# The third group of the second layer joins the seven products in blocks 2 to 5, and exp and relu work in G

## The chip, the cores and the metric

The kernel runs on one core of one Trainium2 chip. The metric is the device time of one execution in microseconds; the runs shown have a median of 294.54 us (294.45 to 295.62, three runs). Engines are named as in the profile: PE is TensorE (PEld its weight loads), DVE is VectorE, ACT is ScalarE, POOL is GpSimd, and SP is the engine whose queue issues most DMAs.

## The reference

The inputs are q, k and v of 8 batches, 8 heads, 576 positions and 64 columns, and two weight matrices. A linear attention feeds a two-layer network:

```
q_s = softmax of q over the columns          k_s = softmax of k over the positions
kv  = k_s^T v  (per head)                    x   = q_s kv, heads side by side: 4608 x 512
h   = x @ w_in            (512 x 2048)
g   = h where h > 0, else exp(h) - 1
out = g @ w_out           (2048 x 512)       4608 x 512, float32
```

## The kernel before

**Blocks.** The 4608 rows of x are cut into nine blocks (j = 0 to 8) of 512 rows. The attention of a batch is worked off in 16 half batches (n = 0 to 15): load q, k and v, exp on ACT, sums and normalisation (`stage1`), turning q by a DMA transpose (`turn`), widening (`widen`), the small matmuls (`side`, `kv_mm`, `ao_mm`), and a copy to XT (`xt`), where x lies transposed.

**First layer.** For each block, eight groups g = 0 to 7 of 256 hidden columns each. A group (`hg`, `hg_mm`) is eight matmuls of 512 columns into one half of PSUM's first four banks (`PS[g % 2]`), then exp on ACT from PSUM into a buffer ESB (two of them, in turn), relu(1 - exp) on ACT in ESB, and two DVE instructions that make max(h, 0) - relu(1 - exp) from PSUM and ESB and write it into two units of GR (here called G). So a PSUM half is free for the group after next when the second of these two is done. G has 24 units; a block takes 16 of them, 8 that the pair ts = 1 of the block before last has left and 8 that the pair ts = 0 of the last block has left (`units`).

**Second layer.** Blocks 0 and 1 do it with plain matmuls (`out_mm`). From block 2 on, a block has two pairs (ts = 0, 1) of 256 rows, and `pair` multiplies each by w_out in the manner of Winograd: 2 x 2 quarters, seven products in place of eight. The contraction of 2048 is cut into three groups, `GROUPS = ((0, 4), (4, 6), (6, 8))` in units z of 256. A product of a group is one 256-column matmul per z. The sums that the products need are made beforehand: differences of weights once (`combos`: T1 to T4, of which T2 to T4 in TB and T1 in place in W2), and four sums of G's quarters per pair and group (`sums`: S1 and A11 - A21; `late`: A11 - S1 and A12 less that), on POOL, each of (z1 - z0) x 128 columns.

In blocks 2 to 5 only groups 0 and 1 take part in the seven products (`groups(j)`); the third group (z = 6, 7) is done by `std`: four 512-column matmuls for each of the two 128-row tiles of a pair. From block 6 (`WHOLE`) on, the third group takes part too, with its weight differences in TB2 and its sum in SB2, two buffers that lie over RAW, free by then.

DVE adds the products up from PSUM (`dve` in `pair`, L871), ACT copies two quarters from PSUM (`copy`, L876), and SP stores the rows (`store`).

**Order.** Each engine's order is written out by hand as lists of operation numbers (`ORDER`, found by a planner beforehand). `Sched.add` notes what each operation reads and writes, and `emit` issues each engine's list in order with a semaphore wait where an operation depends on another engine's. So an engine works strictly in the order of its list: an operation that waits holds everything behind it. The planner's own times are used only to place a few warming matmuls at the start (`fill`).

Of the kernel before, what the change touches and what calls it, by code (L numbers as in the profile page):

```python
# [21 lines left out]
NSP = 6  # L22
# [78 lines left out]
class Op:  # L101
    __slots__ = ("eng", "dur", "emit", "deps", "key", "idx", "start", "end",
                 "dma", "sem", "val", "clock", "nbytes", "follow", "side", "late", "packet", "margin",
                 "gate", "span", "behind", "early")

    def __init__(self, eng, dur, emit, key, dma=None, nbytes=0):
        self.eng, self.dur, self.emit, self.key = eng, dur, emit, key
        self.deps = {}
        self.dma, self.nbytes = dma, nbytes
        self.start = self.end = None  # L110
        self.behind, self.early = None, 0
        self.follow, self.side, self.packet, self.margin = None, 0, 4608, 0


class Sched:
# [4 lines left out]
    LAND = 350  # L120
    SPIN_FROM, WARM = 5500.0, 11300.0
    FIRST = {"sp": 2050, "act": 2050, "gp": 2700}
    DMA_RATE = 385.0

    def __init__(self, nc):
        self.nc = nc
        self.E = {"sp": nc.sync, "act": nc.scalar, "dve": nc.vector,
                  "pe": nc.tensor, "gp": nc.gpsimd}
        self.ops = []
        self.w = {}  # L130
        self.r = {}
        self.gate = None

    def add(self, eng, dur, emit, key, R=(), W=(), X=(), dma=None, nbytes=0, after=(),
            follow=None, side=0):
        op = Op(eng, dur, emit, key, dma, nbytes)
        op.idx = len(self.ops)
        op.follow, op.side, op.late, op.gate = follow, side, False, self.gate
# [22 lines left out]
    def order(self):  # L161
        line = {e: [self.ops[int(i)] for i in ORDER[e].split()] for e in self.ENG}
        free = {e: 740.0 for e in self.ENG}
        queue = {e: 0.0 for e in self.ENG}
        seq = []
        while any(line.values()):
            before = len(seq)
            for e in self.ENG:
# [104 lines left out]
def t_f32r(n):  # L273
    return (n + 32) / 2.4
# [881 lines left out]
```

## Time and profile before

| | |
|---|---|
| median of three runs | 294.54 us |
| profiled execution, first to last instruction | 292.2 us, 5351 instructions |
| 8 matmuls of a first-layer group, L637 | 576 in all, 142.7 us busy |
| plain second layer, L698 (blocks 0 and 1) | 128, 32.4 us |
| seven products, L850 | 672 of 256 columns |
| third group, L863 (std) | 64 of 512 columns, 17.3 us |
| GR written on DVE, L676 | 120 of 512 columns, 689 ns each |
| adding products on DVE, L871 | 84, 417 ns each |
| exp and relu on ACT, L653 and L673 | 72 and 64, 1025 and 1060 ns each |
| sums on POOL, L798 | 256 columns some 745 ns, 512 columns some 1300 ns |
| longest waits | DVE for relu 55.7 us (46 times), ACT for the first layer's matmuls 36.9 us (43 times), DVE's adds for products 25.7 us (27 times) |
| loads of k, q, v on SP's queue, from issue to landing | 6.1, 5.0, 5.4 us in the median |

The page gives no time of the profiled execution beside its span; the median of the runs is 2.3 us above it. Waits of DVE, ACT and POOL cost nothing as long as PE does not wait for them in turn. Matmuls overlap, so a group's mean duration (393 ns for L637) is more than its share of time: 142.7 us for 576 is 248 ns each, and the distance between pieces of the chain is nearer still.

### The profile page before, as it was taken

Reading aid. Unit: us, or ns where it says so; the run is one execution under the profiler, and the core shown is the slowest. Engines: PE = TensorE matmul, PEld = TensorE weight load, DVE = VectorE, ACT = ScalarE, POOL = GpSimd, SP = SyncE. Lnnn points to the kernel's source line nnn. Section 1 sums busy time; section 2 is a strip of 40 time slices with the busy share of each in tenths; the row PEclk is TensorE's granted clock in tenths of the full one; section 3 lists DMA queues with packets and bytes.
Section 4 is the critical chain, followed back from the end, with each engine's and each line's share of the span. In section 5 each row is a group of like instructions: output and inputs, shape, how many; then the busy total and the mean of one; then the engine's idle time right before and its main releaser. Section 6 shows DMA issues by size and latency. Waiting matters only on the chain.

```text
span 292.2 us, 5351 instructions
## 1 busy us (share of the span) xinstructions
PE 282.1 (97%) x2128; PEld 242.1 (83%) x2128; DVE 177.4 (61%) x326; ACT 211.3 (72%) x249; POOL 220.6 (76%) x216
## 2 busy tenths in 40 slices
PE   2899999999999999999999999999999999999994
PEld 0478887778888888888988888988989889988994
DVE  3748834787464686575656675756542667356753
ACT  4858849988998989786976779856883667665610
POOL 1992435617788999899786979799678968899880
PEclk9999999999999999999999999999999999999999
DMA  7999999799995679577919476403111010400235
GB/s 254 397 367 388 389 389 335 169 281 332 274 316 125 101 232 159 168 182 254 234 45 207 150 157 202 98 16 77 38 36 36 2 31 5 110 0 2 55 90 144
DMA packets 36472, 50.01 MB, mean 171 GB/s; under 512 B 16352, under 2 KB 18144, under 8 KB 36448
## 3 DMA queue, kind: packets, MB, share of 16 engines
q1 hardware_dynamic: 29680, 33.96, 43.5%
q0 software_dynamic: 6528, 15.47, 17.6%
q10 hardware_dynamic: 240, 0.26, 0.4%
q8 instruction: 16, 0.26, 0.4%
q14 instruction: 8, 0.07, 0.1%
HBM read 36.70 MB, written 9.44 MB: 158 GB/s over the span
## 4 chain that ended last, share of the span: by engine, by line
PE 94%; DMA 2%; POOL 2%; SPq 0%; issue 0%; DVE 0%
PE PS L637 46%; PE PS L850 28%; PE PS L698 10%; PE PS L863 5%; PE PS L552 3%; DMA KR<-in_k_dram 2%; PE PS L521 2%; POOL W L379 1%; POOL VB L418 0%; PE PS L465 0%; POOL QS L441 0%; SPq L359 0%; PE PS L564 0%; DVE OSB L871 0%
## 5 line engine op out<-in xcount | busy, mean ns | idle before, releaser
L637 PE MATMUL PS<-XT,W 128*128 128x512 f32 x576 | 142.7, 393 | 0.1
L676 DVE SCALAR_TENSOR_TENSOR GR<-PS,ESB 128x512 fp32r<-128x512 f32 (+1 forms) x124 | 87.5, 705 | 59.6 <-ACT ESB L673 55.7
L637 PEld LDWEIGHTS PS<-XT,W 128*128 128x128 f32 x576 | 105.0, 188 | 21.5 <-DMA W<-in_moe_w_in_dram 0.5
L653 ACT ACTIVATE ESB<-PS 128x1024 f32<-128x1024 f32 x72 | 73.5, 1025 | 38.4 <-PE PS L637 36.9
L673 ACT ACTIVATE ESB<-ESB 128x1024 f32<-128x1024 f32 x64 | 67.8, 1060 | 1.5
L798 POOL TENSOR_TENSOR GR<-GR 128x512 fp32r<-128x512 f32 (+1 forms) x65 | 62.7, 982 | 5.5 <-PE PS L850 4.9
L871 DVE TENSOR_TENSOR OSB<-OSB,PS 128x256 f32<-128x256 f32 x84 | 34.6, 417 | 26.9 <-PE PS L850 25.7
L850 PE MATMUL PS<-W,GR 128*128 128x256 f32 x288 | 45.5, 284 | 0.0
L850 PE MATMUL PS<-TB,GR 128*128 128x256 f32 x288 | 43.8, 283 | 0.0
L441 POOL TENSOR_TENSOR QS<-QR,RZQ 128x1152 f16<-128x1152 f32 (+1 forms) x16 | 30.2, 1886 | 17.2 <-DVE RZQ L433 16.5
L850 PEld LDWEIGHTS PS<-W,GR 128*128 128x128 f32 x288 | 40.8, 190 | 2.0
L850 PEld LDWEIGHTS PS<-TB,GR 128*128 128x128 f32 x288 | 39.9, 191 | 1.7
L798 POOL TENSOR_TENSOR SB<-GR 128x256 fp32r<-128x256 f32 (+1 forms) x31 | 30.0, 973 | 11.4 <-DVE GR L676 10.4
L698 PE MATMUL PS<-W,GR 128*128 128x512 f32 x128 | 32.4, 395 | 0.0
L798 POOL TENSOR_TENSOR GR<-SB,GR 128x256 fp32r<-128x256 f32 (+1 forms) x31 | 29.9, 978 | 2.4 <-PE PS L850 1.9
L418 POOL CAST VB<-VR 128x1152 bf16<-128x1152 f32 (+1 forms) x16 | 17.7, 1106 | 16.1 <-DMA VR<-in_v_dram 16.1
L698 PEld LDWEIGHTS PS<-W,GR 128*128 128x128 f32 x128 | 23.4, 188 | 4.7 <-DVE GR L683 0.2
L430 DVE TENSOR_REDUCE ZQ<-QR 128x18 f32<-128x1152 f32 (+2 forms) x18 | 21.8, 1209 | 6.5 <-ACT QR L428 4.9
L586 ACT ACTIVATE XT<-PS 128x512 fp32r<-128x512 f32 (+6 forms) x32 | 19.2, 603 | 6.8 <-PE PS L552 3.0
L876 ACT ACTIVATE OSB<-PS 128x256 f32<-128x256 f32 x28 | 10.4, 377 | 18.3 <-PE PS L850 9.3
L402 ACT ACTIVATE KR<-KR 128x1152 bf16<-128x1152 f32 x16 | 18.4, 1157 | 0.8 <-DMA KR<-in_k_dram 0.8
L398 ACT ACTIVATE QR<-QR 128x1152 f32<-128x1152 f32 x14 | 16.3, 1161 | 1.5 <-DMA QR<-in_q_dram 1.5
(57 smaller groups left out, 220.4 us busy)
## 6 DMA issues: line engine op xcount, KB each, us to landing
out_dram<-OSB SPq DMA_DIRECT2D x61, 128.0 KB, 2.4
QR<-in_q_dram SPq DMA_DIRECT2D x12, 576.0 KB, 5.0
KR<-in_k_dram SPq DMA_DIRECT2D x12, 576.0 KB, 6.1
VR<-in_v_dram SPq DMA_DIRECT2D x12, 576.0 KB, 5.4
W<-in_moe_w_out_dram POOLq DMA_DIRECT2D x4, 1024.0 KB, 16.6
QR<-in_q_dram POOLq DMA_DIRECT2D x4, 576.0 KB, 12.1
VR<-in_v_dram POOLq DMA_DIRECT2D x4, 576.0 KB, 13.0
KR<-in_k_dram POOLq DMA_DIRECT2D x4, 576.0 KB, 11.1
```

The source lines that it names most:

```text
L402: S.add("act", t_act(1152, False), lambda e: e.activation(ek[:, :, :, :].rearrange("p h c d -> p (h c d)"), flat(k), AF.Exp), key - 2, X=[ ...
L430: S.add("dve", t_dve(m), lambda e, qp=qp, zp=zp: e.tensor_reduce(zp, qp, AX.X, ALU.add), key - 3, R=[f"qR{i}{x}" for x in xs], W=[f"ZQ{i}{ ...
L441: lambda e, qp=q[:, :, a:b, :], rz=rz, dst=qs[:, :, a:b, :]: e.tensor_tensor(dst, qp, rz, ALU.mult),
L586: S.add("act", t_act((h1 - h0) * n_, True), lambda e, dst=dst, src=src: e.activation(dst, src, AF.Copy), key, W=W, X=X)
L637: last = e.matmul(P[:, t * 512:(t + 1) * 512], self.W1[:, kc, tt * 128:(tt + 1) * 128], self.XT[:, kc, rc:rc + BLK], start=(kc == 0), stop ...
L653: S.add("act", t_act(1024, True), lambda e: e.activation(esb[:, :], self.PS[ps][:, :], AF.Exp), key, W=[f"E{i}"], X=banks)
L673: S.add("act", t_act(1024, False), lambda e: e.activation(esb[:, :], esb[:, :], AF.Relu, bias=1.0, scale=-1.0), key, X=[f"E{i}"])
L676: S.add("dve", t_dve(512 if j else 1024), lambda e, u=u: e.scalar_tensor_tensor(*(x[:, :, u, :] if j else x for x in (gt, P)), 0.0, ev[:, ...
L698: last = e.matmul(dst, self.tile(jb, jj, ts), self.W2[:, jj, c0:c1], start=(jj == 0), stop=(jj == 15))
L798: lambda e: e.tensor_tensor(dst, a, b, op), key, R=R, W=W, X=X, after=after)
L850: last = e.matmul(dst, a[i][:, y_, :], b[i][:, y_, :], start=start and i == 0 and y_ == 0, stop=stop and i == len(grps) - 1 and y_ == z - ...
L871: S.add("dve", t_dve(256), lambda e: e.tensor_tensor(dst, a, b, ALU.add), key, R=R, W=W, X=X, after=after)
```

## The change

Four things change together.

1. `pair` uses all three groups in every block from 2 on; `std` is gone. The weight differences of the third group are made in block 2 with those of the others, in a TB that has eight columns of units in place of six (`NSP`), and its sums lie in SB. TB2 and SB2 are gone. To make room, the ESB buffers, which only blocks 0 and 1 still use, lie over TB.
2. From block 2 on, exp and relu write into the units of G that will take the group's result, by a second name GE for the same memory; DVE then writes the result over them.
3. Some operations may be done by either of two engines: weight differences and sums on POOL or DVE, copies from PSUM on ACT or DVE, casts of v and widening of q on ACT or POOL, normalisation on POOL or DVE. The engine is the one in whose list the operation stands (`home`).
4. The lists are new from the middle of block 1 on. `order` is simpler, and notes that only it used (`follow`, `gate`, `margin`) are gone.

The counts of matmuls, from the two orders: L863's 64 of 512 columns are gone, and the seven products have 784 of 256 columns in place of 672. DVE has 421 instructions for 326, ACT 238 for 251 (its DMA issues among them), POOL 166 for 216. Of the sums, POOL had 133 and DVE 3; POOL has 99 and DVE 69.

```diff
-NSP = 6
+NSP = 8
...
+        self.home = {int(i): e for e, line in ORDER.items() for i in line.split()}
...
     def add(self, eng, dur, emit, key, R=(), W=(), X=(), dma=None, nbytes=0, after=(), side=0):
+        alts = eng if isinstance(eng, dict) else {}
+        if alts:
+            eng = self.home.get(len(self.ops))
+            eng = eng if eng in alts else next(iter(alts))
+            dur = alts[eng]
...
+    def copy(self, e, dst, src):
+        return e.activation(dst, src, AF.Copy) if e is self.nc.scalar else e.tensor_copy(dst, src)
...
+        self.GE = nc.alloc_sbuf_tensor_at("GE", [128, 24, 2, 256], F32, offset=nc.sbuf_base - 49152)
...
     def hg(self, j, g, ps, key, how, whole=True):
-        i = self.eslot % len(self.ESB)
-        self.eslot += 1
-        esb = self.ESB[i]
-        S.add("act", t_act(1024, True), lambda e: e.activation(esb[:, :], self.PS[ps][:, :], AF.Exp), key,
-              W=[f"E{i}"], X=banks)
+        own = gw
+        if j < 2:
+            i = self.eslot % 2
+            self.eslot += 1
+            own = [f"E{i}"]
+            ge = self.ESB[i][:, :].rearrange("p (c u t) -> p c u t", c=2, u=2) if j else self.ESB[i][:, :]
+        S.add("act", t_act(1024, True), lambda e: e.activation(ge, P, AF.Exp), key, W=own, X=banks)
...
     def pair(self, j, ts, key):
-        grps = self.groups(j)
-        full = 2 in grps
+        grps, tail = (0, 1, 2), j >= WHOLE
...
         def second():
-            if not full:
-                std(0, 2 * NSP, 16, False)
+            pass
...
     def add_sum(self, grp, dst, a, b, op, key, R, W, X, after):
-        self.S.add(eng, n_ * 2.4 + 60 if eng == "gp" else t_dve(n_),
+        self.S.add({"gp": n_ * 2.4 + 60, "dve": t_dve(n_)}, None,
...
                     if g == 7:
-                        self.combos(key, 0)
-                        self.combos(key, 1)
+                        for grp in range(3):
+                            self.combos(key, grp)
                         self.sums(2, 0, key, (0, 1))
```

More of the change, by code (lines that the diff above doesn't have):

```diff
@@ L102 @@
     __slots__ = ("eng", "dur", "emit", "deps", "key", "idx", "start", "end",
-                 "dma", "sem", "val", "clock", "nbytes", "follow", "side", "late", "packet", "margin",
-                 "gate", "span", "behind", "early")
+                 "dma", "sem", "val", "clock", "nbytes", "side", "early", "alts")
     def __init__(self, eng, dur, emit, key, dma=None, nbytes=0):
@@ L110, in __init__ @@
         self.start = self.end = None
-        self.behind, self.early = None, 0
-        self.follow, self.side, self.packet, self.margin = None, 0, 4608, 0
+        self.side = self.early = 0
 class Sched:
@@ L163, in order @@
         free = {e: 740.0 for e in self.ENG}
-        queue = {e: 0.0 for e in self.ENG}
-        seq = []
+        queue, seq = 0.0, []
         while any(line.values()):
-            before = len(seq)
+            ready = []
             for e in self.ENG:
-                while line[e]:
+                if line[e] and all(d.end is not None for d in line[e][0].deps):
                     o = line[e][0]
-                    near = [d for d in (o.follow, o.gate, o.behind) if d is not None]
-                    if any(d.end is None for d in list(o.deps) + near):
-                        break
-                    t = max([free[e]] + [d.end + self.hop(d, o) for d in o.deps] +
-                            [d.start + (d.dur if d.eng == e else 0) for d in near[:2] if d is not o.behind])
-                    o.start, o.end = t, t + o.dur
-                    free[e] = o.end
-                    if o.dma:
-                        if o.behind is not None:
-                            queue[e] = max(queue[e], o.behind.end - self.LAND - o.behind.margin)
-                        queue[e] = max(t + self.FIRST[e], queue[e]) + o.nbytes / self.DMA_RATE
-                        o.end = queue[e] + self.LAND + o.margin
-                    seq.append(line[e].pop(0))
-            assert len(seq) > before
-        rank = {o: i for i, o in enumerate(seq)}
-        return self.fill(sorted(seq, key=lambda o: (o.start, rank[o])))
+                    ready.append((max([free[e]] + [d.end + self.hop(d, o) for d in o.deps]), e))
+            t, e = min(ready)
+            o = line[e].pop(0)
+            o.start, o.end = t, t + o.dur
+            free[e] = o.end
+            if o.dma:
+                queue = o.end = max(t + self.FIRST[e], queue) + o.nbytes / self.DMA_RATE
+            seq.append(o)
+        return self.fill(seq)
     def hop(self, d, o):
@@ L198, in fill @@
             if o.eng == "pe" and not done:
-                count = int((o.start - free - 20) / 430 if free < self.WARM else
+                count = int((o.start - free - 20) / 421 if free < self.WARM else
                             (o.start - free - 150) / 260)
@@ L301, in alloc @@
         self.XT = a("XT", [128, 4, RING], F32R)
-        self.ESB = [a(f"ESB{i}", [128, 1024], F32) for i in range(2)]
         self.OSB = [a(f"OSB{i}", [128, 512], F32) for i in range(2)]
@@ L318, in alloc @@
         self.VR1 = at("VR1", [128, 2, CH, D], F32, offset=base + 6912)
+        self.ESB = [at(f"ESB{i}", [128, 1024], F32, offset=tbase + NSP * 1024 + 4096 * i)
+                    for i in range(2)]
         self.OSB0 = [at(f"OSBX{i}", [128, 512], F32, offset=tbase + 2048 * i)
@@ L381, in load_w1 @@
             W=[f"W1_{g}{kc}" for g in range(g0, g1) for kc in kcs],
-            dma=f"w1{g0}{kcs[0]}", nbytes=len(kcs) * (g1 - g0) << 17, after=after, follow=self.ident)
-        self.S.ops[-1].margin = 300
+            dma=f"w1{g0}{kcs[0]}", nbytes=len(kcs) * (g1 - g0) << 17, after=after)
     def load_w2(self, s, key, after=()):
@@ L404, in stage1 @@
                 key - 2, X=[f"kR{i}"])
[L405 to L407 removed]
+            for h0, h1, x in ((0, 5, ""), (5, 9, "y")) if vconv == "pair" else ((0, 2, ""),):
                 if vconv == "pair":
@@ L436, in stage1 @@
             for a, b, ys in cuts:
-                eng = "gp" if n in self.BYPOOL and ys == [1] or n in self.ALLPOOL else "dve"
                 m = (b - a) * 128
+                cost = {"gp": m * 2.0 + 30, "dve": t_dve(m)}
+                if n in self.BYPOOL and ys == [0]:
+                    cost = {"dve": t_dve(m), "gp": m * 2.0 + 30}
                 rz = self.RZQ[i][:, :, a:b].unsqueeze(3).broadcast_to([128, 2, b - a, D])
-                S.add(eng, m * 2.0 + 30 if eng == "gp" else t_dve(m),
+                S.add(cost, None,
                       lambda e, qp=q[:, :, a:b, :], rz=rz, dst=qs[:, :, a:b, :]: e.tensor_tensor(
@@ L470, in tp @@
             W = [f"qsT{self.alt(n)}{x}" for x in W]
-            if eng == "act":
-                S.add("act", t_act(n_, True), lambda e, dst=dst, src=src: e.activation(
-                    dst, src, AF.Copy), key, W=W, X=X, after=after)
-            else:
-                S.add("dve", t_dve(n_), lambda e, dst=dst, src=src: e.tensor_copy(dst, src),
-                      key, W=W, X=X, after=after)
+            cost = {"act": t_act(n_, True), "dve": t_dve(n_)}
+            S.add(dict(sorted(cost.items(), reverse=eng == "dve")), None,
+                  lambda e, dst=dst, src=src: self.copy(e, dst, src), key, W=W, X=X, after=after)
     def turn(self, n, key):
@@ L758, in combos @@
         z0, z1 = GROUPS[grp]
-        if grp == 2:
-            early = [f"qR0{x}" for x in range(2)] + ["kR0"]
-        else:
-            early = [f"Ox{i}{x}" for i in range(4) for x in "LR"]
-        old, hi = [f"B{grp}"], grp == 2
-        for s, (dst, a, b, W, X, R) in enumerate((
-                (T3, B22, B12, [f"T1{grp}"] + early, [], self.w2(grp)),
-                (T1, B12, B11, [f"T3{grp}"] + [] if hi else [f"T3{grp}"] + self.w2(grp), [], []),
-                (T2, B22, T1, [f"T0{grp}"], [], [f"T3{grp}"]),
-                (T4, B21, T2, [f"T2{grp}"], [], [f"T0{grp}"]))):
-            S.add("gp", (z1 - z0) * 256 * 2.34 + 30, lambda e, dst=dst, a=a, b=b: e.tensor_tensor(
-                dst, a, b, ALU.subtract), key, R=R, W=W, X=X, after=S.ops[-1:] if s == 1 else S.r["qR00"][-1:] if hi and s == 0 else ())
-    def groups(self, j):
-        return (0, 1, 2) if j >= WHOLE else (0, 1)
+        early = [f"Ox{i}{x}" for i in range(z0 // 2, z1 // 2) for x in "LR"]
+        for s, (dst, a, b, W, R) in enumerate((
+                (T3, B22, B12, [f"T1{grp}", f"E{min(grp, 1)}"], self.w2(grp)),
+                (T1, B12, B11, [f"T3{grp}"] + self.w2(grp), []),
+                (T2, B22, T1, [f"T0{grp}"] + early, [f"T3{grp}"]),
+                (T4, B21, T2, [f"T2{grp}"], [f"T0{grp}"]))):
+            n_ = (z1 - z0) * 256
+            S.add({"gp": n_ * 2.34 + 30, "dve": t_dve(n_)}, None, lambda e, dst=dst, a=a, b=b: e.tensor_tensor(
+                dst, a, b, ALU.subtract), key, R=R, W=W, after=S.ops[-1:] if s == 1 else ())
     def sb(self, j, ts, grp):
@@ L805, in sums @@
             S1, N = self.sb(j, ts, grp)
-            own = [f"T1{grp}"] if grp == 2 and (j, ts) != (NBLK - 1, 1) else []
-            one = self.add_sum(grp, S1, A21, A22, ALU.add, key, h + g + own, N, [], self.summed.get(N[0], []))
+            one = self.add_sum(grp, S1, A21, A22, ALU.add, key, h + g, N, [], self.summed.get(N[0], []))
             self.third[j, ts, grp] = self.add_sum(grp, A21, A11, A21, ALU.subtract, key, m, [], h, [one])
@@ L823, in pair @@
         end = (j, ts) == (NBLK - 1, 1)
-        grps = self.groups(j)
-        full = 2 in grps
-        b0, b1 = (6, 7) if ts and full else (4, 5)
+        grps, tail = (0, 1, 2), j >= WHOLE
+        b0, b1 = (6, 7) if ts and tail else (4, 5)
         H = [self.bank(b)[:, c:c + 256] for c in (0, 256) for b in (b0, b1)]
-        if full:
+        if tail:
             x, y, over = 2 * ts, 2 * ts + 1, []
@@ L856, in mms @@
                       R=list(names[i]) + ([f"T{wnames}{grp}"] if wnames is not None else self.w2(grp)))
-        def std(p, jj0, jj1, stop):
-            bk = (b0, b1)[p]
-            def mm(e):
-                for jj in range(jj0, jj1):
-                    last = e.matmul(self.bank(bk), self.tile(j, jj, 2 * ts + p), self.W2[:, jj, :],
-                                    start=False, stop=stop and jj == jj1 - 1, skip_group_check=True)
-                return last
-            S.add("pe", (jj1 - jj0) * t_f32r(512), mm, key, side=2, X=[f"b{bk}"],
-                  R=self.gnames(j, ts, range(jj0 // 2, jj1 // 2)) + [
-                      f"W2_{s}" for s in range(jj0 // 4, (jj1 + 3) // 4)])
         def dve(dst, a, b, R, W, X, after=()):
@@ L908, in fourth @@
         def fourth():
-            if not full:
-                std(1, 2 * NSP, 16, False)
-            elif not end:
+            if not end:
                 dve(XR, XR, H[3], [], [], [f"O{x}R", f"b{b1}"])
@@ L914, in fourth @@
             dve(XL, XL, H[1], [], [], [f"O{x}L", f"b{b1}"])
-            if not full:
-                dve(XR, XR, H[3], [], [], [f"O{x}R", f"b{b1}"])
             if end:
@@ L1110, in program @@
                         n_ = (j - 1 + ts, 1 - ts)
-                        self.sums(*n_, key, self.groups(j - 1) if ts == 0 else (0, 1))
+                        self.sums(*n_, key, (0, 1, 2) if ts == 0 else (0, 1))
                 key += 1
```

136 lines of the change are left out of this document (43 added, 93 removed), and 120 rows, old and new, of the table ORDER.

## The prediction, made before the changed kernel ran

> **What bounds the kernel now.** I read the busy times of the engines first, then the chain that ended last, then the groups by shape, then the waits, and last the places where sums run on two engines at once.
>
> ```profile
> PE 282.1 (97%) x2128; PEld 242.1 (83%) x2128; DVE 177.4 (61%) x326; ACT 211.3 (72%) x249; POOL 220.6 (76%) x216
> ...
> PEclk9999999999999999999999999999999999999999
> ...
> PE 94%; DMA 2%; POOL 2%; SPq 0%; issue 0%; DVE 0%
> ```
>
> TensorE is busy 97% of the span, at the full granted clock, and the chain that ended last is TensorE for 94% of it. Busy alone would not do, since matmuls overlap. So I read the chain in order of time: how far apart its pieces start is what a matmul costs.
>
> ```profile
> 215.17 1.84 PE PS L637 x8
> 217.01 1.19 PE PS L850 x10
> 218.21 0.93 PE PS L863 x4
> 219.13 0.95 PE PS L850 x8
> 220.08 1.84 PE PS L637 x8
> ```
>
> No gap lies between the pieces. A 512-column matmul costs 1.84/8 = 0.23 us, a 256-column one 1.19/10 = 0.119 us, so the narrow one is not dearer than half the wide one (0.115) by more than 4%. Over the whole chain I find less than 2 us between pieces from 14 us to 288.6 us. In that stretch the time is the sum of the matmuls, and a change shortens it only by taking matmuls out; any new wait of TensorE comes on top.
>
> **The change part by part.**
>
> *Products.* Blocks 2 to 5 have two pairs each, 8 pairs. Before, the last quarter of the contraction of a pair was done by std (L863): 8 matmuls of 512 columns, 64 in all. In the page's shares by line, L863 holds 5% of the chain, 14.6 us; by pieces it is 64 x 0.23 = 14.7. After, the third group joins the seven products: 7 x 2 matmuls of 256 columns a pair, 112 in all (the order shows 784 matmuls of that line for 672), 112 x 0.119 = 13.3 us. The term is 13.3 - 14.6 = **-1.3 us**. All of it lies on the path.
>
> *Sums of the third group.* Each pair makes 4 sums of 256 columns more: 32. No sum is on the chain now. The sums also move: POOL had 133 and VectorE 3; after, POOL has 99 and VectorE 69 (45 of 256 columns, 24 of 512). POOL gives VectorE also 4 of the 12 weight differences and 3 normalisations, and ScalarE 6 casts of V and 3 widenings of q; ScalarE gives VectorE 14 output copies and 9 copies to XT. By the rows' means POOL loses some 60 of its 220.6 us, ScalarE stays within 3 us of 211, and VectorE gains 18 (new 256-sums at 0.42) + 16 (512-sums at 0.69, the price of the 512-column row of L676, nearest in size) + 20 (copies, normalisations, weights) = 54 us: 177 to 231 us, 79% of the span.
>
> *Where that is tightest.* In block 4 of the new order VectorE has 58 instructions from one block's last GR write to the next's: 16 GR writes x 0.689, 13 pair sums x 0.417, 9 sums (4.3), 2 reductions x 1.343, a normalisation (1.55 by 859 ns for 640 columns), and 17 small ones and copies (5.6): 30.6 us as durations. Neighbours that do not depend on each other start some 0.08 us before the one ahead ends (262.51 + 1.42 against 263.85 in the timeline), which leaves 26 us at the least. TensorE needs 8 x 1.84 + 112 x 0.119 + 2.4 for attention = 30.4 us. Before, the stretch of block 4 had VectorE busy 20.85 of 33 us:
>
> ```profile
> 129.00:162.00 33.00, 33.00 (x329) 29.18 (x328) 20.85 (x42) 24.89 (x30) 27.72 (x26) 1.00 0.71 190
> ```
>
> (The columns after the length are TensorE, weight loads, VectorE, ScalarE, POOL.) VectorE goes from 63% to between 86% and 100%: still under TensorE, with little cover.
>
> *What a sum costs when both engines sum.* The trace of before shows this in one place, the tail:
>
> ```profile
> L798 POOL TENSOR_TENSOR GR<-GR x3: 733/1185/1292, 280.8 to 282.7; 128x256 fp32r<-128x256 f32 x2, 128x512 fp32r<-128x512 f32 x1
> L798 DVE TENSOR_TENSOR GR<-GR x3: 417/501/919, 282.4 to 284.1; 128x256 fp32r<-128x256 f32 x2, 128x512 fp32r<-128x512 f32 x1
> ```
>
> (Minimum, median, maximum in ns.) POOL's 256-column sum from 282.7 on lies beside VectorE's sums and takes 1185 ns, where the one ahead of it took 733. VectorE's 512-column sum takes 919 ns against 689 for an L676 of that width, its 256-column one 501 against 417. So a meeting costs POOL 0.45 us and VectorE 0.08 to 0.23 us. The bound for all of VectorE: 42 x 0.08 + 23 x 0.23 = 8.7 us more if every new sum meets a busy POOL, nothing if none does; POOL is busy about half the time after the change, so I take 4 us, spread over 200 us and mostly beside TensorE.
>
> [...]
>
> *In place.* Exp and relu write into the unit of G that the result will take, so exp now waits for that unit and not for one of two ESB buffers. Exp's old wait for a buffer was at most 0.7 us in 2 times (ScalarE's ESB behind VectorE's GR in the waits). The unit is last read by the fourth product of an earlier pair, and the new order has these products ahead of the group's own matmuls on TensorE, which exp awaits anyway. No gain and no loss, 0 +- 0.1 us.
>
> *The chain that frees PSUM.* A group's matmuls end at 271.09; exp, relu and two GR writes follow back to back and end at 274.70: 3.6 us. The group after next needs that PSUM. Counted by pieces, TensorE's work between the end of a group and the start of the one after next is 3.98 us at the least after the change, and 4.18 before; 4.46 or less 13 times after, 16 times before. Where it was 4.2 before, TensorE did not wait. Nothing from this term, 0.2 us less slack at the worst.
>
> *Queues.* The same 119 instructions stand on SP's queue and the same 12 loads of q, k and v on POOL's, but SP's order is new. The tightest load is K of n = 12: it is behind a store of block 3 that waits for a pair sum. By the pieces that sum ends 2.3 us after group 3 of block 4, and the load starts at +2.9. From issue to landing these loads took 5.0 (Q), 5.4 (V) and 6.1 us (K) in the median, 3.8 at best. ScalarE reaches the K exp at +7.0, ahead of the exp of group 5, whose matmuls end at +8.6; group 7 needs its PSUM at +12.7. K landed at +7.9 costs nothing, at +9.0 it pushes the exp of group 5 to +10.1 and group 7 to +13.9: 0 to **1.1 us**, I take 0.4. I found no load with less room.
>
> *Start and end.* The orders agree until the middle of block 1; the last add and the last store are the same. 0.
>
> **Sum:** -1.3 (products) + 0.4 (K load) + 0.25 (a meeting or two that reach TensorE) = -0.65 us. Made against the span, 292.2 - 0.65 = 291.55; the runs' median is 2.3 us above the span, for start and end that the page does not show, so 294.54 - 0.65 = **293.9 us**.
>
> **The rivals.**
>
> *All of it hides:* -1.3, and up to 0.5 of the small gaps of TensorE after 57 us go too. 292.7 to 293.2 us. For it: PSUM slack is as before, POOL has 60 us more room. Against: VectorE's 86%.
>
> *VectorE held by POOL becomes the bound (slower).* One place, in block 4, times from the start of group 2: POOL's chain of five (two sums of 512 columns, two of 256, one normalisation: 2 x 1.3 + 2 x 0.74 + 2.16, less overlaps 6.1 us) starts at -0.5, when a product of block 3 has freed its operand, and ends at 5.6. A VectorE sum waits for it (0.69), and behind that sum on VectorE stands the second GR write of group 2 (0.69), to 7.05. Group 4 needs that PSUM at 7.86: 0.65 us of slack after the signal. One meeting takes 0.45 of it and TensorE does not notice; from the second on it stalls by 0.25, and by 0.7 with a third. If all five blocks 3 to 7 have two such places, ten stalls of 0.25 to 0.7 are 2.5 to 7, net +1.2 to +5.7, about 297 us. For it: VectorE near full, and a cross-engine wait that before did not have. Against: only 69 short sums, and each stall of TensorE gives the others slack for the next.
>
> *The gain is just eaten:* stalls of 1.3 to 2.7 us, 294.6 to 296.0. *The change doesn't do what it says:* if narrow products ran slower than 0.131 us the swap would cost time (64 x 0.23 / 112); the 672 of before stand at 0.119, so I give this nothing of its own.
>
> **How the numbers follow.** About 0.5% (1.5 us) is what a measurement of this kernel can tell from no change; the three runs shown spread over 1.2 us. Forecast, 293.2 to 294.6: 0.47. All hides: 0.15. Eaten: 0.10. VectorE and POOL bound: 0.28. The forecast and "eaten" are within 0.5%, and so is the upper edge of "all hides" but I count that case as faster: faster 0.15, same 0.57, slower 0.28. The range leaves out the lower edge of the first rival and the upper half of the slower one: 292.9 to 297.5 us.
>
> **What would show it.** TensorE's 256-column pieces at 0.119 us, 784 of them, and no L863: the first step right. POOL sums well over 0.75 us and VectorE 512-sums near 0.92: meetings. TensorE or its weight loads idle behind VectorE's GR write or behind ScalarE's exp after a K load: the two stall terms. If TensorE waits in total by more than 3 us, VectorE's cover was too thin and I am wrong; if it waits nowhere, I have counted stalls that are not there.

## The result and the profile after

The changed kernel takes 296.38 us in the median of 21 runs, the kernel before 294.98 us in 21 runs beside it: a ratio of 1.0042 (95% interval 1.0023 to 1.0061), about 1.2 us slower, where I had forecast 0.65 us faster. A second comparison, told of below, gave 1.0016 (0.9986 to 1.0046). The profiled execution of the changed kernel has a span of 295.6 us against 292.2, 3.4 us more than before; as shown below, it met one stall of over a microsecond that most executions don't meet.

These are the lines of the page of the changed kernel that answer to those shown of before: the busy times, the granted clock, and the shares of the chain that ended last.

```profile
PE 282.2 (95%) x2176; PEld 243.4 (82%) x2176; DVE 229.5 (78%) x421; ACT 212.2 (72%) x236; POOL 167.5 (57%) x166
...
PEclk9999999999999999999999999999999999999999
...
PE 74%; DMA 13%; DVE 5%; ACT 4%; SPq 2%; POOL 1%; issue 1%
```

The clock is full in both. TensorE is as busy as before, but only 74% of the chain is TensorE, where it was 94%. What came in is DMA, 13%: transfers now stand in the chain, and that is the line to follow up. A share of the chain is not time lost, since TensorE works beside most of it. Two pieces of the chain of the changed kernel in order of time show that the products cost what they should.

```profile
217.54 1.91 PE PS L803 x16
219.46 1.84 PE PS L617 x8
```

1.91/16 is 0.119 us for a narrow product and 1.84/8 is 0.23 us for a wide matmul, as before. To separate work from waiting I added up, from the first group's first matmul to the last matmul, the distances from each matmul's start to the next, and put aside as **gaps** whatever exceeds the median of its kind by over 25 ns. Before: 269.8 us of work and 4.2 us of gaps. After: 268.5 us and 8.8 us. So the work shrank by 1.4 us, as forecast, and the gaps grew by 4.7 us. Four places of the changed kernel hold 3.7 us of them:

| place in the profile of after | gap | what TensorE waited for |
|---|---|---|
| 58.7 us, block 1 | 1.27 us (0.16 before) | VectorE's write of GR, behind a relu of 1.77 us |
| 117.0 us | 0.63 us | ScalarE's copy to OSB, behind a store |
| 154.4 and 157.7 us, block 4 | 0.86 + 0.52 us | VectorE's copy to OSB behind a store; a GR write behind the exp after the K load |
| 165.0 us | 0.38 us | VectorE's pair sum behind a sum of 0.92 us |

For block 4 the chain tells it in full. It runs, in the changed kernel, from the issue of the K load of n = 12 to the next group's matmuls (start, length, what).

```profile
147.09 6.65 DMA KR<-in_k_dram
153.75 0.02 issue
153.77 1.17 ACT KR L396
154.94 0.92 ACT GE L643
155.85 0.02 issue
155.88 1.07 ACT GE L645
156.95 0.02 issue
156.97 0.70 DVE GR L649
157.67 0.02 issue
157.70 0.70 DVE GR L649
158.40 0.04 issue
158.44 1.63 PE PS L617 x6
```

No engine in it is slow. The load is issued at 147.09, lands 6.65 us later (K loads take 5.9 us in the median here), and each step follows the last without a pause; the chain starts too late. The waits of the same profile name the transfers (who waited for what, us in total, times, longest).

```profile
ACT KR L396 <- DMA KR<-in_k_dram: 4.2, 3, 2.4
ACT OSB L274 <- DMA out_dram<-OSB: 4.1, 5, 2.2
...
DVE OSB L274 <- DMA out_dram<-OSB: 1.6, 1, 1.6
```

The kernel before has one such row for a K load:

```profile
ACT KR L402 <- DMA KR<-in_k_dram: 0.8, 1, 0.8
```

SP's queue shows why this changed; first the changed kernel (start, length of the issue, what).

```profile
143.87 1.68 SPq L356 DMA_DIRECT2D VR<-in_v_dram  x1
145.60 0.47 SPq L356 DMA_DIRECT2D QR<-in_q_dram  x1
146.58 0.47 SPq L699 DMA_DIRECT2D out_dram<-OSB  x1
147.09 0.59 SPq L356 DMA_DIRECT2D KR<-in_k_dram  x1
147.72 2.16 SPq L467 DMA_TRANSPOSE QT<-QS  x1
149.93 0.60 SPq L699 DMA_DIRECT2D out_dram<-OSB  x1
```

The buffer of that K load is free by 133 us: the first experiment issues the load then, and SP does not wait. In the changed kernel it stands behind a V load that waits for a buffer and a store that waits for a pair sum. The last store shown has its data at 146.6 us and is issued at 149.93, behind the transpose; VectorE's copy into its buffer could start only at 155.13. In the order of before the same K load went out at 132.5 us, 10 us ahead of its use; it is the second of these two.

```profile
132.07 0.89 SPq L359 DMA_DIRECT2D KR<-in_k_dram  x2
```

### The profile page after: what moved, and what is told of

Same layout as the page of the kernel before. It is cut to its first block, busy times and chain, and to the rows that moved or that the text cites. A ratio compares the mean times of both kernels' runs of the same rounds, so it can differ in the third digit from the quotient of the medians.

```text
span 295.6 us, 5475 instructions
## 1 busy us (share of the span) xinstructions
PE 282.2 (95%) x2176; PEld 243.4 (82%) x2176; DVE 229.5 (78%) x421; ACT 212.2 (72%) x236; POOL 167.5 (57%) x166
## 4 chain that ended last, share of the span: by engine, by line
PE 74%; DMA 13%; DVE 5%; ACT 4%; SPq 2%; POOL 1%; issue 1%
PE PS L617 36%; PE PS L803 28%; PE PS L670 7%; DMA KR<-in_k_dram 7%; PE PS L535 2%; DMA VR<-in_v_dram 2%; DMA W<-in_moe_w_in_dram 2%; DMA out_dram<-OSB 2%; DVE GR L649 2%; PE PS L504 1%; ACT GE L643 1%; SPq L356 1%; DVE GR L656 1%; DVE ESB L654 1%; ACT ESB L643 1%
## 5 line engine op out<-in xcount | busy, mean ns | idle before, releaser
L649 DVE SCALAR_TENSOR_TENSOR GR<-PS,GE 128x512 fp32r<-128x512 f32 x112 | 77.0, 688 | 26.0 <-ACT GE L645 24.4
L643 ACT ACTIVATE GE<-PS 128x1024 f32<-128x1024 f32 x56 | 57.3, 1023 | 34.6 <-PE PS L617 28.1
L754 POOL TENSOR_TENSOR GR<-GR 128x256 fp32r<-128x256 f32 (+1 forms) x50 | 48.7, 990 | 21.9 <-PE PS L803 13.4
L645 ACT ACTIVATE GE<-GE 128x1024 f32<-128x1024 f32 x56 | 59.4, 1060 | 1.5
L803 PE MATMUL PS<-W,GR 128*128 128x256 f32 x336 | 53.9, 284 | 1.2 <-DVE OSB L274 0.7
L803 PE MATMUL PS<-TB,GR 128*128 128x256 f32 x336 | 51.5, 283 | 0.0
L754 POOL TENSOR_TENSOR SB<-GR 128x256 fp32r<-128x256 f32 (+1 forms) x21 | 20.1, 964 | 19.7 <-DVE GR L649 15.1
L754 DVE TENSOR_TENSOR GR<-GR 128x256 fp32r<-128x256 f32 (+1 forms) x34 | 21.9, 654 | 2.2 <-PE PS L803 2.0
L274 POOL CAST VB<-VR 128x1152 bf16<-128x1152 f32 (+1 forms) x10 | 10.8, 1078 | 19.7 <-DMA VR<-in_v_dram 16.5
L643 ACT ACTIVATE ESB<-PS 128x1024 f32<-128x1024 f32 x16 | 16.1, 1025 | 7.0 <-PE PS L617 5.9
```

Of the source, the lines that this page charges most:

```text
L274: return e.activation(dst, src, AF.Copy) if e is self.nc.scalar else e.tensor_copy(dst, src)
L643: S.add("act", t_act(1024, True), lambda e: e.activation(ge, P, AF.Exp), key, W=own, X=banks)
L645: S.add("act", t_act(1024, False), lambda e: e.activation(ge, ge, AF.Relu, bias=1.0, scale=-1.0), key, X=own)
L649: S.add("dve", t_dve(512 if j else 1024), lambda e, u=u: e.scalar_tensor_tensor(*(x[:, :, u, :] if j else x for x in (gt, P)), 0.0, ge[:, ...
L754: lambda e: e.tensor_tensor(dst, a, b, op), key, R=R, W=W, X=X, after=after)
L803: last = e.matmul(dst, a[i][:, y_, :], b[i][:, y_, :], start=start and i == 0 and y_ == 0, stop=stop and i == len(grps) - 1 and y_ == z - ...
```

## The experiments

Theory Q: the order of SP's list is what cost the gain, through a late K load and late stores. Theory P, the rival of the prediction: VectorE, held by POOL's sums, has become the bound. Ratios are to the kernel before, run beside each.

**One load earlier.**

```
-  578 654 653 595 589 670 441 588 669
+  578 441 654 653 595 589 670 588 669      (SP's list)
```

> The changed kernel with one load moved in SyncE's list: the K load of n=12 (operation 441) is issued right behind the Q load of n=12 (578), where SyncE then waits some 7 us, instead of behind V and Q of n=13. Nothing else differs. Theory Q (the changed kernel lost its gain to transfers that queue on SyncE: the K exponential waits 2.4 us for this load, VectorE's copy to OSB 1.55 us for a store queued behind it, and TensorE loses 0.86 + 0.52 us at 154 to 158 us): ScalarE's wait for KR near 152 us goes, the TensorE gaps at 154 and 158 us shrink by 0.9 to 1.4 us, ratio to the kernel before falls from 1.0042 to about 1.000 (0.998 to 1.001). Theory P (the sums now on VectorE are held by POOL's, and VectorE sets the pace of block 4): the gap moves to the next VectorE wait and the ratio stays at 1.003 to 1.005.

294.32 us, ratio 0.9987 (0.9963 to 1.0011). SP's queue of this kernel:

```profile
132.10 0.60 SPq L356 DMA_DIRECT2D VR<-in_v_dram  x1
132.74 0.50 SPq L356 DMA_DIRECT2D QR<-in_q_dram  x1
133.28 0.49 SPq L356 DMA_DIRECT2D KR<-in_k_dram  x1
140.33 1.11 SPq L699 DMA_DIRECT2D out_dram<-OSB  x2
```

Its span is 291.9 us; there is no gap over 0.15 us between 150 and 160 us, and none at 117. All gaps together are 5.4 us, work 268.3. One number moved in one list takes back 0.55% of the time against the first comparison of the changed kernel and 0.3%, within the intervals, against the second; so theory P is not what made the changed kernel slow. Not all of the better profile is the move's doing: the store whose landing ended the gap at 117 us is issued as before, over 20 us ahead of the first change, and landed 4.18 us after its issue here, 5.41 us in the changed kernel.

**Stores ahead of loads as well.**

```
-  487 331 488         ...  654 653 595 589 670 441 588 669
+  487 488 331         ...  441 654 653 588 595 670 669 589
```

> As the kernel with the early K load, and three more moves in SyncE's list: the K load of n=10 (331) behind the second store of the first pair (488) instead of ahead of it; the store 669 right behind its twin 670 and both ahead of the Q load of n=13 (589); the transpose 588 ahead of the V load 595. Theory Q: the ScalarE copy to OSB near 117 us no longer waits 1.2 us for a store, which gives another 0.6 us: ratio about 0.998 (0.996 to 1.000), and TensorE gaps over 0.3 us are left only where VectorE was held by POOL. Theory P: 1.003 to 1.005.

294.36 us, ratio 0.9972 (0.9946 to 0.9998), as theory Q has it, but not to be told from the kernel with one move alone. The largest gap past block 1 is 0.31 us at 99.5 us, the next 0.26 us at 161.9.

**POOL without sums.**

```
+        if self.S.ops[-1].eng == "gp":
+            self.S.ops[-1].emit = lambda e: e.tensor_copy(dst, a)
```

> The kernel with the four moves on SyncE, and each of the 99 sums of the second layer that POOL does is a copy of the sum's first input of the same size (the additions on POOL are left out). Each keeps its place, its tiles and its waits; a copy reads one input only. Theory P (VectorE's sums stand beside POOL's sums, 0.2 to 1.2 us longer each time, and this costs the time): VectorE's sums fall back to 417 and 689 ns, and the time falls by over 1 us below the kernel with the four moves: ratio 0.993 to 0.995. Theory Q (meetings are hidden but for one gap of 0.38 us): within 0.5 us of the kernel with the four moves, ratio 0.996 to 0.999.

294.15 us, ratio 0.9971 (0.9944 to 0.9997): nothing gained over the four moves. VectorE's sums did become short. First their rows in the changed kernel (busy us, mean ns), then in this one.

```profile
L754 DVE TENSOR_TENSOR GR<-GR 128x256 fp32r<-128x256 f32 x20 | 12.2, 612 | 0.3 <-PE PS L803 0.3
L754 DVE TENSOR_TENSOR GR<-GR 128x512 fp32r<-128x512 f32 x14 | 10.0, 715 | 1.9 <-PE PS L803 1.7
```

```profile
L754 DVE TENSOR_TENSOR GR<-GR 128x512 fp32r<-128x512 f32 x14 | 9.6, 687 | 1.9 <-PE PS L805 1.7
L754 DVE TENSOR_TENSOR GR<-GR 128x256 fp32r<-128x256 f32 x20 | 8.3, 418 | 0.3 <-PE PS L805 0.3
```

The meetings are real, 194 ns more on a 256-column sum in the mean, and hidden as far as these intervals (0.8 us either way) tell; whether they were hidden with the K load late as well was not run. In this kernel's profile other waits come up (1.4 us of gaps from 167 to 173 us, VectorE 1.9 us behind a store), and the relu in block 1 was held again (1.29 us), so that one execution with its span of 294.5 us says less than the median.

**The stall in block 1.** 

```
+        self.ops[227].deps[self.ops[255]] = "raw"
```

> The kernel with the four moves on SyncE, and the POOL product QS of block 1 (operation 227) waits for VectorE's relu on ESB (255), so that it can't be under way when that relu starts; block 1 is otherwise as in both kernels. In the changed kernel's profile the relu took 1.77 us instead of 0.69 because this POOL product had started first, and TensorE lost 1.27 us at 58.7 us; in the profile before it started 0.2 us later and nothing was lost. If that race between the two is lost in a good part of the executions, the median falls by 0.3 to 1.0 us below the kernel with the four moves, and the slowest executions become rarer. If it is rare: the same within 0.2 us. In both cases the relu takes 0.69 us.

294.45 us, ratio 0.9975 (0.9947 to 1.0002): the median is that of the four moves, so the stall is not in most executions. Of the twelve profiles in which it can happen, before and the experiments included, it is in three. What happens is a race. In the changed kernel POOL's product QS starts ahead of VectorE's relu:

```profile
57.22 1.77 DVE L654 TENSOR_SCALAR ESB<-ESB 128x1024 f32<-128x1024 f32 x1 [1.09 <-ACT ESB L643]
```

```profile
56.32 2.12 POOL L430 TENSOR_TENSOR QS<-QR,RZQ 128x1152 f16<-128x1152 f32 x1 [0.44 <-DMA QT<-QS]
```

In the kernel with the four moves it starts 0.05 us behind it:

```profile
57.25 0.69 DVE L654 TENSOR_SCALAR ESB<-ESB 128x1024 f32<-128x1024 f32 x1 [1.09 <-ACT ESB L643]
```

```profile
57.30 2.62 POOL L430 TENSOR_TENSOR QS<-QR,RZQ 128x1152 f16<-128x1152 f32 x1 [1.06 <-DMA QT<-QS]
```

In each, the one that started second paid: the relu 1.08 us, or POOL 0.50 us, and only the first reached TensorE. POOL's start depends on when a transpose has read QS, for which it had waited 0.44 us in the first and 1.06 us in the second. Neither operation is part of the change, and the kernel before runs the same race; in its profile POOL lost it, with 2.49 us from 57.23, where the relu had started at 57.05 and took 0.69. This is most of why the profiled execution of after lies 3.4 us above that of before and the medians only 1.4.

**The changed kernel again.** No edit.

> The changed kernel unaltered, beside the next three kernels. Theory Q (late K load and stores queued behind loads on SyncE): ratio to the kernel before 1.003 to 1.006 again, and its profile shows ScalarE waiting over 1.5 us for the K load of n=12 and TensorE losing over 0.9 us between 150 and 160 us. If these waits were an accident of the one profile, they are absent here while the ratio stays. The 1.27 us at 58.7 us, where POOL's product QS had started ahead of VectorE's relu, may be there or not: neither operation was changed.

296.18 us, ratio 1.0016 (0.9986 to 1.0046). Without the race of block 1 its span is 293.7 us and its gaps are 6.8 us. The ratio is below the 1.003 to 1.006 expected, and the late load is there, smaller than I expected: ScalarE waits 1.27 us for it, TensorE loses 0.38 us at 155.6 us, and nothing at the store of 154. The store of 116 us costs 0.56 us again and the meeting near 163 us 0.38 us. These lines are from its chain.

```profile
145.48 0.47 SPq L699
145.95 0.04 issue
145.99 5.55 DMA KR<-in_k_dram
151.54 0.02 issue
151.56 1.17 ACT KR L396
```

The load's issue follows a store that waits for a pair sum (0.43 us of VectorE just ahead in the chain), as the prediction had it.

**Fewer bytes ahead of the load.**

```
+        if (t, n) == ("v", 13):
+            dst, src = dst[0:32], src[0:32]
```

> The changed kernel, its order untouched, with the V load of n=13 cut to 32 of its 128 partitions (the rest of that input is left out), so that 0.44 of 0.59 MB less lie ahead of the K load of n=12 on the queue. Loads landed here at about 0.19 MB a microsecond, so K lands some 2.3 us earlier, near 151.3 us when ScalarE is ready for it, and the stores behind it too. Theory Q: most of the 1.4 us at 154 to 158 us goes: ratio 0.999 to 1.001. Theory P (the pace of VectorE and POOL): 1.003 to 1.006.

295.67 us, ratio 1.0010 (0.9988 to 1.0033), beside 1.0016 for the changed kernel in the same comparison: within the number that theory Q gave, but not to be told from the changed kernel, and not for the reason given. K took 5.78 us from issue to landing, no less than the 5.55 us with the whole V load ahead; TensorE lost 0.52 us at 156.2 us. So my reading that the bytes of the V load hold K up is not borne out. The Q load between them was whole, so this does not say that nothing ahead of K matters; but in the five profiles with K issued late it landed 5.1 to 6.65 us after its issue, and its use followed from that.

**The load later still.**

```
-  670 441 588 669 598
+  670 588 669 441 598
```

> The changed kernel with the K load of n=12 (441) issued still later: behind the transpose 588 and the store 669 instead of ahead of them. The store then lands about 2 us earlier, the K load 1 to 3 us later. Theory Q with the K load as what sets the delay: the longer wait for KR on ScalarE is passed to TensorE one for one: ratio 1.007 to 1.012. If the late store (VectorE's copy to OSB, TensorE's 0.86 us) is what costs, the kernel gets faster: 1.000 to 1.003. Theory P: no change, 1.003 to 1.006.

297.62 us, ratio 1.0100 (1.0065 to 1.0135). ScalarE's wait for the load is 4.5 us, 3.3 us more than in the changed kernel beside it; TensorE has one gap of 2.9 us there; the time is 0.8%, 2.5 us, longer by the ratios and 1.4 us by the medians. Not all of that is the wait. In this profile the granted clock, 1.00 until then, is 0.50 from 158.6 to 162.1 us, right behind the gap; it is the 7 in the row of the page.

```profile
PEclk9999999999999999999997999999999999999999
```

The four slowest of its nine executions (299.25 to 299.82 us, the profiled one among them) have a mean granted clock of 0.991 to 0.994; the four with 1.000 took 296.83 to 297.62 us, 0.7 to 1.4 us more than the median of the changed kernel beside it. (The ninth, 297.53 us, had 0.993.) So as far as four executions tell, the longer wait costs about that much, well under the 3.3 us, and in other executions a fallen clock comes on top. The store is issued ahead of the load here and nothing is gained by it: the load sets the delay in block 4.

**The store alone.**

```
-  670 441 588 669
+  670 669 441 588
```

> The changed kernel with only the store 669 moved: right behind its twin 670, ahead of the K load of n=12 and the transpose 588. The store lands near 151 us instead of 155, the K load 0.5 us later than before. If the K load sets the delay, the TensorE gap at 154 us goes but the one at 158 us grows by as much: the same or up to 0.5 us slower than the changed kernel, ratio 1.003 to 1.007. If the store sets it: 0.9 us faster, 0.999 to 1.002.

294.87 us, ratio 0.9994 (0.9962 to 1.0027). There is no gap at 154 us, and 0.57 us at 156.4, from the load. But the changed kernel beside it had no gap at 154 either, this one has a gap of 1.06 us at 97.6 us that no other profile shows, and the intervals overlap: the run doesn't tell what the store costs.

**The meeting near 162 us.**

```
-  603 700 604 731
+  603 731 700 604      (VectorE's list, on top of the four moves)
```

> The kernel with the four moves on SyncE and one swap on VectorE: the pair sum into OSB (731), whose product is done by then, goes ahead of the 256-column sum of G (700) and not behind it. In every profile of the changed order, also in those with the moves on SyncE, that sum stood beside a POOL sum and took 0.91 to 0.92 us instead of 0.42, and TensorE lost 0.26 to 0.39 us (near 162 us there) because it needs the bank that the pair sum frees. If this meeting is the whole of that gap, the gap near 162 us goes and the ratio falls by 0.001 below the kernel with the four moves (0.9972 there): 0.995 to 0.998. If the chain goes on behind another wait, the gap comes back within 5 us and the ratio stays.

294.31 us, ratio 0.9984 (0.9955 to 1.0014). The gap at 162 us is gone; the ratio is not below that of the four moves, but 0.3 us is less than such intervals tell. With the block-1 wait of above added:

> As the kernel with the swap on VectorE, and POOL's product QS of block 1 (227) waits for VectorE's relu (255). In the profiles so far POOL had started first in 3 of 9 executions in which it could (relu 1.77 to 1.79 us instead of 0.69, TensorE losing 1.13 to 1.29 us). The median should be that of the kernel with the swap or up to 0.4 us below it, 0.994 to 0.998, and fewer executions should lie over 1 us above the median. If the spread stays as wide, it has another source.

294.12 us, ratio 0.9967 (0.9941 to 0.9993), span 291.9 us, gaps 5.4 us. After block 1 the profile has one gap over 0.15 us, 0.19 us. This version is faster than both kernels, by about 1.0 us than the kernel before. Whether its times spread less can't be said from 12 runs (293.54 to 295.86 here, 293.84 to 295.06 with the four moves).

**How much room VectorE has.** Work that nothing reads is added.

```
+  e.tensor_reduce(self.SCR[:, c:c + z1 - z0], a.bitcast(F32), AX.X, ALU.add)
   return e.tensor_tensor(dst, a, b, op)      (the first 30 sums on VectorE)
```

> The kernel with the four moves on SyncE, and each of the first 30 sums of G that VectorE does (blocks 2 to 5) has a reduction of its first input ahead of it, which nothing reads: some 0.35 us for a sum of 256 columns and 0.6 us for 512, about 13 us more on VectorE between 90 and 200 us. It tells how near VectorE is to being the bound, as the rival of the prediction had it. If VectorE still has cover there: TensorE loses under 1 us more, ratio 0.997 to 1.001. If VectorE has next to none: at least half of the 13 us reaches TensorE, ratio 1.015 to 1.04.

301.63 us, ratio 1.0226 (1.0183 to 1.0270). VectorE is busy 243.2 us, 13.3 us more than the 229.9 us of the kernel with the swap; TensorE's gaps are 12.5 us, 6.4 us more than with the four moves. Four of TensorE's waits in this profile:

```profile
PE PS L811 <- DVE GR L761: 1.6, 1, 1.6
PE PS L811 <- DVE OSB L820: 1.6, 2, 1.2
PE PS L811 <- DVE OSB L274: 1.0, 1, 1.0
PE PS L618 <- DVE GR L650: 0.7, 2, 0.4
```

All four are for VectorE. The time is 7.3 us longer than with the four moves, just over half of the 13.3 us added, which is the case that I had put as "next to none" for cover. VectorE is not the bound in the changed order, since half of the work still hides, but it has little room.

**A late load in the kernel before.** Is a late K load dear only because VectorE is so full?

```
-  438 437 621 622 566 573
+  438 621 622 566 437 573      (SP's list of the kernel before)
```

> The kernel before, with its own order but for one load: the K load of n=12 (437 there) is issued behind the transpose 566, near 140.3 us instead of 132.4, so that it lands 5 to 6 us later than it did (139.6) and ScalarE, which comes to it at 142.8 us, waits some 2 to 3 us, as it did in the first profile of the changed kernel. If a late K load costs TensorE as such: a TensorE gap of 0.4 to 1.5 us near 150 us and 0.3 to 1.3 us more in all, ratio 1.001 to 1.005. If it cost the changed kernel only because VectorE has less cover there (VectorE 63% busy in this stretch before the change): no TensorE gap over 0.3 us near 150 us and ratio 0.998 to 1.001.

296.52 us, ratio 1.0052 (1.0027 to 1.0076): 1.5 us slower, where the changed kernel was 1.2 and 0.5 us slower. ScalarE waits 1.97 us, TensorE loses 0.91 us at 149 us. From its chain:

```profile
140.70 4.53 DMA KR<-in_k_dram
145.23 0.02 issue
145.26 1.17 ACT KR L402
146.42 0.92 ACT ESB L653
...
150.17 1.86 PE PS L637 x7
```

These are the steps of the changed kernel's chain under other line numbers, with one XT copy among them. The late load costs by itself, with two ESB buffers, 672 products and nearly all sums on POOL.

## Why the prediction was wrong

**Products, -1.3: right.** 784 products at 0.119 us; TensorE's time without gaps went from 269.8 us to 268.3 to 268.6 us in six profiles of the new order.

**Sums and busy times: right.** VectorE 229.5 us (231 worked out), POOL 167.5 (some 160), ScalarE 212.2 (within 3 of 211).

**Block 4: right as far as it went.** VectorE's 26 to 30.6 us of TensorE's 30.4 measured 26.6 in 32.1. The answer of the changed kernel to the stretch shown of before, same columns:

```profile
127.90:160.00 32.10, 31.08 (x260) 27.57 (x259) 26.63 (x50) 26.54 (x29) 21.87 (x22) 1.00 0.64 182
```

TensorE's 31.08 busy of 32.10 leave 1.0 us idle there, in the two gaps. With the early load alone the same stretch takes 30.50 us, against 30.4 by the pieces. The added work shows that the lower end, 86%, was no promise of cover.

**Meeting price, 0.25 us on the path: right in sum by luck, wrong in mechanism.** I took 0.08 to 0.45 us a meeting from the tail. In the profile the second to start was held until the first had ended: a 256-column sum on VectorE took 1497 ns, 1214 of them beside a POOL sum that had started first and 283 after it. The sums on VectorE lost 7.2 us by their rows (4 taken, 8.7 the bound); one meeting near 163 us reached TensorE, for 0.26 to 0.39 us in the profiles that have it, and with POOL's sums gone the time stayed.

**In place, 0, and the chain that frees PSUM, nothing: not contradicted.** In the profile with the early load no gap past block 1 exceeds 0.28 us, and TensorE waits for no exp or GR write there. No run undid the in-place writing alone, so a small cost remains possible.

**Queues, +0.4: the step that failed.** It named the right load and the right cause, "behind a store of block 3 that waits for a pair sum". The transfers as a whole cost more than the term, and the term looked at one load. In size: 0.4 us was taken for the load, and as a gap of TensorE behind the load's exp that is what four profiles with the load late show, 0.38 to 0.57 us. But moving the load ahead of what it never needed to follow made the kernel 0.55% faster by the first comparison and 0.3% by the second (1.0042 and 1.0016 against 0.9987; the second lies within the intervals): 0.9 to 1.6 us. The store behind it on the queue cost 0.86 us more in one profile; what else makes up the difference the profiles don't settle. In extent: "I found no load with less room" looked at loads alone. The stores have due times too, since a result buffer is refilled, and a late one held a copy, a PSUM bank, and TensorE: 0.56 to 0.67 us at 117 us in three of the six profiles that have this store behind a K load (it took 5.2 to 5.4 us to land in these, 4.0 to 4.9 in the others), and 0.86 at 154 in one. The row that showed it was there before the change, ScalarE's copy waiting 5.9 us in 6 times for stores; I took it as hidden because TensorE had not waited then.

The store issued at 111.98 behind a K load took 5.41 us to land, where stores took 2.4 us in the median; put ahead of that load, in the second experiment, it took 2.38. Behind the load it took 4.0 to 5.4 us in six profiles, so its place on the queue cost it 1.6 to 3.0 us; what holds it back there no run shows.

**Start and end, 0: right for the change**, but the race in block 1 lies in that part: 1.1 us more in three of ten profiles of the new order. In the two of the old order POOL came second and TensorE lost nothing over 0.2 us.

**The sum.** By the profile: -1.36 of work, +1.39 load and store of block 4, +0.63 store, +0.38 meeting, +1.11 race, +1.2 in small gaps, and 0.1 at the two ends: 3.4 us. Without the race and with the second profile's 0.38 in place of 1.39 it is some +1.3, near the first comparison's +1.2 and above the second's +0.5. The small gaps (at 100 us a GR group behind a cast of V that ScalarE now does, 0.31 us; attention near 173 us, 0.31 us in some profiles) had no term in my sum, and no run took them apart.

**The rivals.** The time fell in the range of "the gain is just eaten" (294.6 to 296.0 from a start of 294.54), to which I gave 0.10. "VectorE held by POOL" had the sign but not the cause: with the four moves made, removing POOL's sums gained nothing, and one load moved brought the time back. Its premise, VectorE near full, was right by the added work. And "if TensorE waits by more than 3 us, VectorE's cover was too thin" was a bad test: TensorE's gaps grew by 4.7 us, for reasons of which most had nothing to do with VectorE's load.

## What to carry to other kernels

When an order is solved anew, list for every DMA, loads and stores alike, when its buffer is free, when it is issued, when it lands and when it is first needed, and compare that list before and after: a load that goes out some 11 us later than it could (behind the Q load issued at 135.2 us, instead of at 147.1) is found in a minute, and moving it takes one number in a list. A buffer that is refilled makes a store a deadline, so stores that share a queue with loads belong in front of loads that have time (5.41 us to land behind a K load here, 2.38 ahead of it). Where a wait of TensorE grows to some 3 us (2.9 in the one profile that shows a fallen clock behind it), read the granted clock behind it before the time is put down to the wait. Look at more than one profile before a gap is put down to a change: here a race between two untouched instructions moved a microsecond from one execution to the next.

## What the runs showed of the hardware

VectorE's relu and sums, which work in SBUF, and POOL's two-input work held each other up in these profiles: the one that started second got on only when the first had ended. A relu on VectorE that met POOL's QS took 1774 ns, 1222 beside it and 552 after it, against 694 alone; a POOL QS behind the relu took 2617 ns against 2122. In both, all but some 0.14 us of the second one's own time came after the first had ended, and so with the sum of 1497 ns. In the profile of the changed kernel 13 sums of 256 columns on VectorE started 270 to 1214 ns ahead of the end of a two-input instruction of POOL; they ended 280 to 287 ns behind that end, where such a sum takes 418 ns without POOL's sums. VectorE's writes of GR, which read PSUM and one SBUF tile, were untouched there: 79 beside POOL's two-input work had a mean of 687 ns, 33 with none beside them 689. What holds the second one back the runs do not show.

TensorE's granted clock stayed at 1.00 through gaps of up to 1.8 us (the longest in the kernel with added work) and fell to 0.50 for 3.4 us behind the one of 2.9 us. One profile shows this, and no run here varied the gap alone.

A load of 0.59 MB took 4.5 to 6.65 us from issue to landing in these places (8.0 us for the early K load, the third of three issued within 1.2 us), and cutting 0.44 MB from the load two places ahead of it in the queue did not shorten that (5.78 us against 5.55). What sets it is open.
